# A cross network of six layers: bias load on GpSimd's queue with early bias products, and tail weights laid by copies

## The chip, the cores and the metric

The kernel runs on one core of a Trainium2 chip. The metric is the device time of one execution in microseconds, the median of several runs. A core has a matrix engine (TensorE, PE in the profile), a vector engine (VectorE, DVE), an activation engine (ScalarE, ACT), GpSimd (POOL) and SyncE (SP), which only issues transfers. DMA transfers can be issued from SP, ACT and GpSimd; each has a queue of its own.

## The reference

`x0` is 4096 x 416, `ws` is 6 x 416 x 416, `bs` is 6 x 416, all bf16. The output is the last `x`.

```python
def reference(x0, ws, bs):
    x = x0
    for l in range(ws.shape[0]):
        x = x0 * (x @ ws[l] + bs[l]) + x
    return x
```

## The kernel before, in words

**Layout.** Rows of the batch are worked in four passes `p` of 1024 rows, each as two blocks `blk` of 512. The features stand on partitions, so `x` is kept transposed. The 416 features are three chunks of 128 (index `k` as input, `m` as output) and a tail of 32. The tail of a pass's 1024 rows is packed on 128 partitions as four groups of 32, each group holding 256 rows (`x0t_sb`, `xt_sb`), so the 32 tail rows of a weight matrix must stand four times, once on each group's partitions: that is `w3_sb[:, l, :]`. The tail-to-tail part of the weights, 32x32, stands four times on the diagonal of a 128x128 matrix of zeros, `wc_sb[:, l, :]`.

**Biases.** PSUM keeps the sum of all layers' products, and `x` after layer l is x0 times (1 + all products so far + all biases so far). The sums of the biases come out of seven small products: `bsa_sb` (a row of ones and the six rows of `bs`) against the 7x6 triangle `u_sb`. They land in PSUM bank 7 and DVE copies them to `cb_sb` (L562); every later step on DVE and ACT reads it as its scalar, and `cl_sb` on GpSimd (L275) is made from it for the last layer.

**Steps of a layer.** `n = p*6 + l`. PE does `main(p, l, 0, n)` (chunk to chunk, block 0), `tail` (tail to chunks, L464; tail to tail, L398 with `wc_sb`; chunks to tail, L485) and `main(p, l, 1, n)`. DVE multiplies the results by `x0` (L579, L588), ACT and GpSimd share one chunk (L661, L285), and ACT copies the tail's other order (L627) and the next layer's `wc_sb` blocks (`corner`, L623). All order is written out by hand: each engine has its own list of instructions and waits on counting semaphores.

**The start**, around which the change lies. PE's list begins with `idle(28)`, matmuls on constants with no use for their result, then a wait for four set-up instructions of GpSimd (`s_setup`), and then `first()`:

- `turn(c)` for c = 0, 1, 2: twelve transposes (L316) of the first 512 rows, which wait for the two loads of `xin_sb`, the one on SP's queue, the other on ACT's.
- `biases()`: the seven products, which wait for `s_bs`, the load of `bs`.
- chunk k = 0 of layer 0 for block 0 (L388), which waits for the weights `s_w0[k]` and for DVE's copies of the turned rows into `x0T_sb` (L557, `s_ev`).
- two transposes of the tail (L359), which wait for GpSimd's packing `xtn_sb` (L262).
- `four_tails()`: one matmul of `rep_sb`, a 32x128 matrix of four identities side by side, with `w30_sb`, the 32 tail rows of layer 0's weights. It puts four copies of them in PSUM; ACT copies these to `w3_sb[:, 0, :]` (L630, `s_w30`), and then ACT and GpSimd copy two diagonal blocks of `wc_sb` each (L623 and L272, `s_wc` and `s_wc0`).
- chunks k = 1 and k = 2. Then `tail(0, 0, 0)` begins, with L464.

For layers 1 to 5 the four copies of the tail rows come from a DMA with a broadcast source (L174).

ACT's queue issues, in this order: second half of `xin_sb`, `xtb_sb` (tails of rows 512 to 1023), `bs`, `w30_sb`. GpSimd issues no DMA; its list begins with the memset of `ones_sb`, the row of ones, `ident`, `u_sb`, `rep_sb` and the zeros of `wc_sb`. SP's queue issues the first half of `xin_sb`, the three chunks of layer 0's weights, a transposing load of rows 512 to 1023, then the other weights and passes.

Of the kernel before, what the change touches and what calls it, by code (L numbers as in the profile page):

```python
# [7 lines left out]
ALU = mybir.AluOpType  # L8
ACTF = mybir.ActivationFunctionType


def bass_standalone__dcn_v2_cross__recsys_kernel(
# [13 lines left out]
    B, D = x0.shape  # L26
    L = ws.shape[0]
    DF = 384
    DR = D - DF
# [10 lines left out]
    with ExitStack() as es:  # L40
        block = es.enter_context(nc.Block())

        def sb(name, shape, dt=BF16):
            return es.enter_context(nc.sbuf_tensor(name, shape, dt))

        w_sb = sb("w_sb", [128, L, 3, D])
        w3_sb = sb("w3_sb", [128, L, D])
        w30_sb = sb("w30_sb", [DR, D])
        rep_sb = sb("rep_sb", [DR, 128])
        wc_sb = sb("wc_sb", [128, L, 128])  # L50
        x0T_sb = sb("x0T_sb", [128, 3, B])
        x0t_sb = sb("x0t_sb", [128, NP, 2, NT])
# [15 lines left out]
        ones_sb = sb("ones_sb", [128, 128])  # L68
        bsa_sb = sb("bsa_sb", [L + 1, D])
        u_sb = sb("u_sb", [L + 1, L])  # L70
        cb_sb = sb("cb_sb", [128, 4, L], FP32)
        ps = es.enter_context(nc.psum_tensor("ps", [128, 8, NB], FP32))
# [14 lines left out]
        def swapped(ap):  # L87
# [1 line left out]
            return [  # L89
                (ap[64 - 64 * h:128 - 64 * h, 1, :], ap[64 * h:64 * h + 64, 0, :]) for h in range(2)  # L90
            ]

        def blocks(l):

            gs = [slice(32 * g, 32 * g + 32) for g in range(4)]
            return [(wc_sb[g, l, g], w3_sb[g, l, DF:D]) for g in gs]

        def four(l):

# [8 lines left out]
        s_ones, s_setup, s_g = sem("s_ones"), sem("s_setup"), sem("s_g")  # L108
# [128 lines left out]

        @block.gpsimd
        def _(pool):
            pool.memset(ones_sb[:, :], 1.0).then_inc(s_ones, 1)  # L240
            pool.memset(bsa_sb[0:1, :], 1.0).then_inc(s_setup, 1)
            pool.wait_ge(s_ones, 1)
            pool.affine_select(
                out=ident[:, :], in_=ones_sb[:, :], pattern=[[-1, 128]],
                compare_op=ALU.is_equal, fill=0.0, base=0, channel_multiplier=1,
            ).then_inc(s_setup, 1)
            pool.affine_select(
                out=u_sb[:, :], in_=ones_sb[0:L + 1, 0:L], pattern=[[1, L]],
                compare_op=ALU.is_ge, fill=0.0, base=1, channel_multiplier=-1,
            ).then_inc(s_setup, 1)  # L250
            pool.affine_select(
                out=rep_sb[:, :].rearrange("f (g e) -> f g e", e=DR),
                in_=ones_sb[0:DR, :].rearrange("f (g e) -> f g e", e=DR),
                pattern=[[0, 4], [-1, DR]], compare_op=ALU.is_equal, fill=0.0, base=0,
                channel_multiplier=1,
            ).then_inc(s_setup, 1)
            pool.memset(wc_sb[:, :, :], 0.0).then_inc(s_g, 1)

            for h, src in enumerate((xin_sb[:, :, DF:D], xtb_sb[:, :, :])):
                for x in (s_xin, (s_xtb,))[h]:  # L260
                    pool.wait_ge(x, 16)
                pool.tensor_copy(  # L262
                    out=xtn_sb[:, 0, :, :].rearrange(
                        "b c (h k f) -> b c h k f", h=2, f=DR
                    )[:, :, :, h, :],
                    in_=src.rearrange("b (h c) f -> b c h f", c=2),
                ).then_inc(s_xtp, 1)
            pool.wait_ge(s_xtp, 2)
            pool.wait_ge(s_g, 1)
            pool.wait_ge(s_w30, 1)  # L270
            for o, i in blocks(0)[2:]:
                pool.tensor_copy(out=o, in_=i).then_inc(s_wc0, 1)  # L272
            pool.wait_ge(s_wc0, 2)
            pool.wait_ge(s_cb, 1)
            pool.tensor_scalar(  # L275
                out=cl_sb[:, :, :], in0=cb_sb[:, :, L - 1:L], scalar1=-1.0, scalar2=None,
                op0=ALU.add,
            ).then_inc(s_cl, 1)
            for p in range(NP):
                for l in range(L):  # L280
                    n = p * L + l
                    if n == N1:
                        continue
                    pool.wait_ge(s_act, n + 1)
                    pool.tensor_tensor(  # L285
                        out=xdst(p, l, 0, 2), in0=t_sb[:, n % 2, :], in1=x0c(p, 0, 2),
                        op=ALU.mult,
                    ).then_inc(s_pl, 1)

            pool.wait_ge(s_xr, 16)  # L290
            for i, j in enumerate((2, 3)):
                pool.wait_ge(s_tt, i + 1)
                pool.tensor_tensor(
                    out=o_sb[:, (NP - 1) * TT + j, :], in0=t_sb[:, i, 0:D], in1=xr_sb[:, j, :],
                    op=ALU.mult,
                ).then_inc(s_op, 1)

        @block.tensor
        def _(pe):

            def idle(n):
                ones = nc.const_aps.tensor(1.0, [128, 128], BF16)
                for _ in range(n):
                    pe.matmul(ps[:, 0, 0:128], lhsT=ones, rhs=ones, start=True, stop=True)  # L304

            idle(28)
            pe.wait_ge(s_setup, 4)
            def at(c, j):

                return 4 if (c, j // 2) == (0, 1) else (2, 3, 6)[c]  # L310
# [1 line left out]
            def turn(c):  # L312
# [7 lines left out]
                    if c == 0 and j == 1:  # L320
                        ins.then_inc(s_inT, 1)
                ins.then_inc(s_inT, 1)

            def four_tails():

                pe.wait_ge(s_wt[0], 16)
                whole(ps[:, 3, 0:D], rep_sb[:, :], w30_sb[:, :], True, True).then_inc(s_inT, 1)

            def biases():
                pe.wait_ge(s_bs, 16)  # L330
# [13 lines left out]

            def first():

                for c in range(3):
                    turn(c)
                biases()
                for k in range(3):  # L350
                    pe.wait_ge(s_w0[k], 16)
                    pe.wait_ge(s_ev, k + 2)
                    for m in range(3):
                        for o, x in pieces(0, m, xsrc(0, 0, 0, k)):
                            whole(o, w_sb[:, 0, k, m * 128:(m + 1) * 128], x, k == 0, False)
                    if k == 0:
                        pe.wait_ge(s_xtp, 2)
                        for c in range(2):
                            ins = pe.transpose(  # L359
                                out=psT[:, 2, c * 128:(c + 1) * 128],  # L360
                                in_=xtn_sb[:, 0, c, :], identity=ident[:, :],
                            )
                        ins.then_inc(s_inT, 1)
                        pe.wait_ge(s_ev, 3)
                        four_tails()

            def pieces(blk, m, x):

# [18 lines left out]
            def whole(out, lhsT, rhs, start, stop):  # L387
                return pe.matmul(  # L388
                    out, lhsT=lhsT, rhs=rhs, start=start, stop=stop, skip_group_check=True
                )  # L390
# [54 lines left out]
            def tail(p, l, n):  # L445
                if n == 0:
                    pe.wait_ge(s_ev, 5)
                    pe.wait_ge(s_cb, 1)
                    pe.wait_ge(s_w30, 1)
                elif l == 0:  # L450
                    pe.wait_ge(s_x0t[p], 16)
                elif n < L:
                    pe.wait_ge(s_wt[l], 16)
# [19 lines left out]
                ins.then_inc(s_pe, 1)  # L473

                if n == 0:
                    pe.wait_ge(s_wc0, 2)
                if n < L:
                    pe.wait_ge(s_wc, 4 * n + 2)
                columns(ps_tail, wc_sb[:, l, :], xt[:, 0, :], start=False, stop=False)

                if n == 0:
# [70 lines left out]

        @block.vector
        def _(dve):
            for i, (c, j0, j1) in enumerate(((0, 0, 2), (0, 2, 4), (1, 0, 4), (2, 0, 4))):
                dve.wait_ge(s_inT, i + 1)
                dve.tensor_copy(  # L557
                    out=x0T_sb[:, c, j0 * 128:j1 * 128],
                    in_=psT[:, (2, 4, 3, 6)[i], j0 * 128:j1 * 128],
                ).then_inc(s_ev, 1)  # L560
            dve.wait_ge(s_inT, 5)
            dve.tensor_copy(  # L562
                out=cb_sb[:, :, :],
                in_=ps[:, 7, D:D + 32].rearrange("p (c e) -> p c e", e=8)[:, :, 0:L],
            ).then_inc(s_cb, 1)
            dve.wait_ge(s_inT, 6)
            dve.tensor_copy(out=x0t_sb[:, 0, 0, :], in_=psT[:, 2, 0:NT]).then_inc(s_ev, 1)
            dve.wait_ge(s_ev, 5)
# [37 lines left out]
        def _(act):  # L606
# [3 lines left out]
            act.dma_start(  # L610
                xtb_sb[:, :, :], x0[NB:2 * NB, DF:D].rearrange("(j b) d -> b j d", b=128)
            ).then_inc(s_xtb, 16)
            act.dma_start(bsa_sb[1:L + 1, :], bs[:, :]).then_inc(s_bs, 16)
            act.dma_start(w30_sb[:, :], ws[0, DF:D, :]).then_inc(s_wt[0], 16)

            act.wait_ge(s_ones, 1)
            act.activation(out=act_sb[:, :], in_=ones_sb[:, 0:1], func=ACTF.Identity)

            def corner(l):
                if l > 0:  # L620
                    act.wait_ge(s_wt[l], 16)
                for o, i in blocks(l)[:2 if l == 0 else 4]:
                    act.activation(out=o, in_=i, func=ACTF.Copy).then_inc(s_wc, 1)  # L623

            def other(ap):
                for o, i in swapped(ap):
                    act.activation(out=o, in_=i, func=ACTF.Copy).then_inc(s_dup, 1)  # L627

            act.wait_ge(s_inT, 7)
            act.activation(  # L630
                out=w3_sb[:, 0, :], in_=ps[:, 3, 0:D], func=ACTF.Copy
            ).then_inc(s_w30, 1)
            act.wait_ge(s_g, 1)
            act.wait_ge(s_w30, 1)
            corner(0)

            def sums(n):

# [76 lines left out]
```

## Time and profile before

| what | value |
|---|---|
| median of 3 runs | 129.96 us (129.84 to 130.22) |
| profiled execution | 130.26 us |
| its span | 128.5 us |
| PE busy | 124.4 us (97% of the span) |
| DVE busy | 92.3 us (72%) |
| ACT busy | 45.9 us (36%) |
| POOL busy | 32.0 us (25%) |

The span is the stretch in which the profile shows work; the rest of the profiled execution's time, 1.76 us, lies around it. Engine names are those above; PEld is the loading of the matrix engine's weights, which overlaps its matmuls. `L398` is line 398 of the kernel. Matmuls are pipelined, so the duration of one is longer than the distance from its start to the start of the next. Durations come from one profiled execution, the median from unprofiled runs of the same kernel.

### The profile page before, as it was taken

To read this page: it belongs to the slowest core of one execution; us is meant where nothing else is said; L and a number is where in the kernel's file an instruction comes from. 1 tells how busy PE (TensorE), PEld (TensorE's weight loads), DVE (VectorE), ACT (ScalarE), POOL (GpSimd) and SP (SyncE) were. 2 spreads that over 40 slices of the span, in tenths; PEclk is the share of its full clock that TensorE was granted. 3 is DMA by queue.
4 is the path that set the end of the run, shared out by engine and by line. 5 is a ranking of instruction groups with operands and counts; after the bars stand their busy time and mean duration, and the time that the engine had idled before them with its cause. 6 is when DMAs were issued, how large, how long until landed. Compare 5 with 4: busy or idle time off the path is not lost.

```text
span 128.5 us, 5801 instructions
## 1 busy us (share of the span) xinstructions
PE 124.4 (97%) x2929; PEld 66.2 (52%) x2402; DVE 92.3 (72%) x152; ACT 45.9 (36%) x101; POOL 32.0 (25%) x40
## 2 busy tenths in 40 slices
PE   7999999999999999999999999999999999999990
PEld 7654554555445545545545545545545545546660
DVE  0439669669669669669679678688687697696482
ACT  1345446436404314314404224224214224225920
POOL 6123303303303203213113123123023033033050
PEclk9999999999999999999999999999999999999999
DMA  3979659665969940496300968000000857000026
GB/s 107 267 196 246 171 118 112 123 66 113 116 197 163 122 88 15 85 145 181 114 15 10 133 122 265 5 0 5 5 10 15 161 122 233 5 5 0 0 67 203
DMA packets 35463, 13.27 MB, mean 103 GB/s; under 512 B 26826, under 2 KB 35440, under 8 KB 35440
## 3 DMA queue, kind: packets, MB, share of 16 engines
q1 hardware_dynamic: 34436, 12.52, 48.7%
q10 hardware_dynamic: 1004, 0.38, 1.1%
q8 instruction: 21, 0.34, 1.1%
q14 instruction: 2, 0.02, 0.0%
HBM read 3.99 MB, written 3.41 MB: 58 GB/s over the span
## 4 chain that ended last, share of the span: by engine, by line
PE 97%; DVE 0%; issue 0%
PE ps L398 61%; PE ps L378 11%; PE ps L464 8%; PE ps L388 7%; PE ps L485 6%; PE ps L304 2%; PE ps L316 1%; DVE o_sb L600 0%; PE ps L528 0%; PE ps L332 0%; PE ps L338 0%; PE ps L359 0%
## 5 line engine op out<-in xcount | busy, mean ns | idle before, releaser
L579 DVE SCALAR_TENSOR_TENSOR xT_sb<-ps,cb_sb,x0T_sb 128x512 bf16<-128x512 f32 x100 | 69.3, 743 | 22.5 <-PE ps L464 22.5
L398 PE MATMUL ps<-xT_sb,w_sb 128*32 128x512 bf16 (+1 forms) x1380 | 75.7, 343 | 0.0
L398 PEld LDWEIGHTS ps<-xT_sb,w_sb 128*32 128x32 bf16 x1380 | 37.1, 97 | 35.0 <-issue 8.1
L285 POOL TENSOR_TENSOR xT_sb<-t_sb,x0T_sb 128x512 bf16<-128x512 f32 x20 | 23.3, 1163 | 72.0 <-ACT t_sb L661 72.0
L661 ACT ACTIVATE t_sb<-ps,cb_sb 128x512 f32<-128x512 f32 x23 | 15.8, 687 | 60.0 <-PE ps L464 60.0
L378 PE MATMUL ps<-xT_sb,w_sb 128*32 128x256 bf16 x444 | 26.6, 273 | 0.0
L627 ACT ACTIVATE xt_sb<-xt_sb 64x256 bf16<-64x256 bf16 x38 | 15.8, 415 | 9.8 <-DVE xt_sb L588 9.3
L398 PE MATMUL ps<-x0T_sb,w_sb 128*32 128x512 bf16 (+1 forms) x252 | 14.1, 344 | 0.0
L579 DVE SCALAR_TENSOR_TENSOR xo_sb<-ps,cb_sb,x0T_sb 128x512 bf16<-128x512 f32 x15 | 10.4, 743 | 3.3 <-PE ps L464 3.3
L398 PEld LDWEIGHTS ps<-x0T_sb,w_sb 128*32 128x32 bf16 x252 | 6.7, 97 | 6.5 <-issue 1.5
L464 PE MATMUL ps<-xt_sb,w_sb 32*128 32x256 bf16 x228 | 9.6, 271 | 0.0
L485 PE MATMUL ps<-xT_sb,w_sb 128*32 128x256 bf16 x228 | 9.5, 273 | 0.0
L588 DVE SCALAR_TENSOR_TENSOR xt_sb<-ps,cb_sb,x0t_sb 128x256 bf16<-128x256 f32 x20 | 9.5, 475 | 0.0
L464 PEld LDWEIGHTS ps<-xt_sb,w_sb 32*128 32x128 bf16 x228 | 4.2, 92 | 6.2 <-issue 6.1
L285 POOL TENSOR_TENSOR xo_sb<-t_sb,x0T_sb 128x512 bf16<-128x512 f32 x3 | 3.5, 1164 | 11.2 <-ACT t_sb L661 11.2
L485 PEld LDWEIGHTS ps<-xT_sb,w_sb 128*32 128x32 bf16 x228 | 6.1, 96 | 0.1
L398 PE MATMUL ps<-xt_sb,wc_sb 128*32 128x256 bf16 x76 | 5.6, 283 | 0.0
L623 ACT ACTIVATE wc_sb<-w_sb 32x32 bf16<-32x32 bf16 x22 | 5.0, 227 | 0.6
L388 PE MATMUL ps<-w_sb,xT_sb 128*128 128x416 bf16 x24 | 5.0, 339 | 0.0
L378 PE MATMUL ps<-x0T_sb,w_sb 128*32 128x256 bf16 x84 | 5.0, 273 | 0.0
L600 DVE SCALAR_TENSOR_TENSOR o_sb<-ps,xr_sb 128x416 bf16<-128x416 f32 x6 | 3.3, 585 | 2.4 <-PE ps L528 2.3
L557 DVE COPY x0T_sb<-ps 128x256 bf16<-128x256 bf16 (+1 forms) x4 | 1.4, 358 | 4.5 <-PE ps L316 4.3
(54 smaller groups left out, 48.3 us busy)
## 6 DMA issues: line engine op xcount, KB each, us to landing
out_dram<-o_sb SPq DMA_DIRECT2D x3, 832.0 KB, 4.9
w_sb<-in_ws_dram SPq DMA_DIRECT2D x5, 312.0 KB, 5.5
w_sb<-in_ws_dram SPq DMA_DIRECT2D x8, 104.0 KB, 3.4
xr_sb<-in_x_dram SPq DMA_DIRECT2D x1, 832.0 KB, 6.4
out_dram<-o_sb SPq DMA_DIRECT2D x3, 208.0 KB, 2.1
xin_sb<-in_x_dram SPq DMA_DIRECT2D x1, 208.0 KB, 3.0
xin_sb<-in_x_dram ACTq DMA_DIRECT2D x1, 208.0 KB, 3.3
x0T_sb<-in_x_dram SPq DMA_TRANSPOSE x13, 4.2
```

What stands on the lines that cost most here:

```text
L285: pool.tensor_tensor(out=xdst(p, l, 0, 2), in0=t_sb[:, n % 2, :], in1=x0c(p, 0, 2), op=ALU.mult,).then_inc(s_pl, 1)
L378: return pe.add_instruction(mybir.InstMatmult(name="I-%d" % (1000000 + count[0]), engine=mybir.EngineType.PE, start_tensor_calc=start, sto ...
L388: return pe.matmul(out, lhsT=lhsT, rhs=rhs, start=start, stop=stop, skip_group_check=True)
L398: ins = pe.matmul(out[c:c + 32, :], lhsT=lhsT[:, c:c + 32], rhs=rhs, start=start, stop=stop, skip_group_check=True, tile_position=(0, c),)
L464: ins = pe.matmul(part(blk, m, h ^ other), lhsT=w3_sb[32 * g:32 * g + 32, l, m * 128:(m + 1) * 128], rhs=xt[32 * g:32 * g + 32, other, :], ...
L485: ins = pe.matmul(ps_tail[32 * g:32 * g + 32, :], lhsT=w_sb[:, l, k, DF:D], rhs=xsrc(p, l, g % 2, k)[:, (g // 2) * NT:(g // 2 + 1) * NT], ...
L579: dve.scalar_tensor_tensor(out=halves(xdst(p, l, blk, c)), in0=chunk2(blk, c), scalar=cb_sb[:, c, l:l + 1], in1=halves(x0c(p, blk, c)), op ...
L588: dve.scalar_tensor_tensor(out=tdst(p, l), in0=ps_tail, scalar=cb_sb[:, 3, l:l + 1], in1=x0t_sb[:, p, 0, :], op0=ALU.add, op1=ALU.mult,).t ...
L600: dve.scalar_tensor_tensor(out=o_sb[:, (NP - 1) * TT + j, :], in0=ps[:, BANK[j], 0:D], scalar=1.0, in1=xr_sb[:, j, :], op0=ALU.add, op1=AL ...
L623: act.activation(out=o, in_=i, func=ACTF.Copy).then_inc(s_wc, 1)
L627: act.activation(out=o, in_=i, func=ACTF.Copy).then_inc(s_dup, 1)
L661: act.activation(out=halves(t_sb[:, n % 2, :]), in_=chunk2(0, 2), func=ACTF.Identity, bias=cb_sb[:, 2, l:l + 1],).then_inc(s_act, 1)
```

## The change

The load of `bs` is issued first on GpSimd's queue, no longer third on ACT's, so `w30_sb` becomes ACT's third transfer. The seven bias products stand ahead of the turns, the copy of `cb_sb` is the first in DVE's list, and there are 24 idle products instead of 28. `rep_sb`, `four_tails` and ACT's copy out of PSUM are gone: as soon as `w30_sb` is there, ACT copies it to the first three groups of `w3_sb` and DVE to the fourth, and GpSimd copies all four blocks of `wc_sb` for layer 0 straight from `w30_sb`, each behind the one before. ACT's `corner` is used for layers 1 to 5 only.

```diff
@@ gpsimd
+            pool.dma_start(bsa_sb[1:L + 1, :], bs[:, :]).then_inc(s_bs, 16)
             pool.memset(ones_sb[:, :], 1.0).then_inc(s_ones, 1)
...
-            pool.affine_select(
-                out=rep_sb[:, :].rearrange("f (g e) -> f g e", e=DR),
...
-            pool.wait_ge(s_w30, 1)
-            for o, i in blocks(0)[2:]:
-                pool.tensor_copy(out=o, in_=i).then_inc(s_wc0, 1)
-            pool.wait_ge(s_wc0, 2)
+            pool.wait_ge(s_wt[0], 16)
+            for g in range(4):
+                gs = slice(32 * g, 32 * g + 32)
+                pool.tensor_copy(out=wc_sb[gs, 0, gs], in_=w30_sb[:, DF:D]).then_inc(s_wc0, 1)
+                pool.wait_ge(s_wc0, g + 1)
@@ tensor
-            idle(28)
-            pe.wait_ge(s_setup, 4)
+            idle(24)
+            pe.wait_ge(s_setup, 3)
...
-            def four_tails():
-
-                pe.wait_ge(s_wt[0], 16)
-                whole(ps[:, 3, 0:D], rep_sb[:, :], w30_sb[:, :], True, True).then_inc(s_inT, 1)
...
             def first():
 
+                biases()
                 for c in range(3):
                     turn(c)
-                biases()
...
-                        pe.wait_ge(s_ev, 3)
-                        four_tails()
@@ tail
-                    pe.wait_ge(s_w30, 1)
+                    pe.wait_ge(s_w30, 4)
...
-                    pe.wait_ge(s_wc0, 2)
-                if n < L:
-                    pe.wait_ge(s_wc, 4 * n + 2)
+                    pe.wait_ge(s_wc0, 4)
+                elif n < L:
+                    pe.wait_ge(s_wc, 4 * n)
@@ vector
+            dve.wait_ge(s_inT, 1)
+            dve.tensor_copy(
+                out=cb_sb[:, :, :],
+                in_=ps[:, 7, D:D + 32].rearrange("p (c e) -> p c e", e=8)[:, :, 0:L],
+            ).then_inc(s_cb, 1)
             for i, (c, j0, j1) in enumerate(((0, 0, 2), (0, 2, 4), (1, 0, 4), (2, 0, 4))):
-                dve.wait_ge(s_inT, i + 1)
+                dve.wait_ge(s_inT, i + 2)
...
-            dve.wait_ge(s_inT, 5)
-            dve.tensor_copy(
-                out=cb_sb[:, :, :],
...
+            dve.wait_ge(s_wt[0], 16)
+            dve.tensor_copy(out=w3_sb[96:128, 0, :], in_=w30_sb[:, :]).then_inc(s_w30, 1)
@@ scalar
-            act.dma_start(bsa_sb[1:L + 1, :], bs[:, :]).then_inc(s_bs, 16)
             act.dma_start(w30_sb[:, :], ws[0, DF:D, :]).then_inc(s_wt[0], 16)
...
-            act.wait_ge(s_inT, 7)
-            act.activation(
-                out=w3_sb[:, 0, :], in_=ps[:, 3, 0:D], func=ACTF.Copy
-            ).then_inc(s_w30, 1)
-            act.wait_ge(s_g, 1)
-            act.wait_ge(s_w30, 1)
-            corner(0)
+            act.wait_ge(s_wt[0], 16)
+            for g in range(3):
+                act.activation(
+                    out=w3_sb[32 * g:32 * g + 32, 0, :], in_=w30_sb[:, :], func=ACTF.Copy
+                ).then_inc(s_w30, 1)
```

More of the change, by code (lines that the diff above doesn't have):

```diff
@@ L48, in bass_standalone__dcn_v2_cross__recsys_kernel @@
         w30_sb = sb("w30_sb", [DR, D])
-        rep_sb = sb("rep_sb", [DR, 128])
         wc_sb = sb("wc_sb", [128, L, 128])
@@ L91, in swapped @@
             ]
-        def blocks(l):
-            gs = [slice(32 * g, 32 * g + 32) for g in range(4)]
-            return [(wc_sb[g, l, g], w3_sb[g, l, DF:D]) for g in gs]
         def four(l):
@@ L249, in _ @@
                 compare_op=ALU.is_ge, fill=0.0, base=1, channel_multiplier=-1,
-            ).then_inc(s_setup, 1)
-            pool.affine_select(
-                out=rep_sb[:, :].rearrange("f (g e) -> f g e", e=DR),
-                in_=ones_sb[0:DR, :].rearrange("f (g e) -> f g e", e=DR),
-                pattern=[[0, 4], [-1, DR]], compare_op=ALU.is_equal, fill=0.0, base=0,
-                channel_multiplier=1,
             ).then_inc(s_setup, 1)
@@ L560, in _ @@
                 ).then_inc(s_ev, 1)
-            dve.wait_ge(s_inT, 5)
-            dve.tensor_copy(
-                out=cb_sb[:, :, :],
-                in_=ps[:, 7, D:D + 32].rearrange("p (c e) -> p c e", e=8)[:, :, 0:L],
-            ).then_inc(s_cb, 1)
+            dve.wait_ge(s_wt[0], 16)
+            dve.tensor_copy(out=w3_sb[96:128, 0, :], in_=w30_sb[:, :]).then_inc(s_w30, 1)
             dve.wait_ge(s_inT, 6)
@@ L619, in corner @@
             def corner(l):
[L620 to L623, printed above, removed]
+                act.wait_ge(s_wt[l], 16)
+                for g in range(4):
+                    gs = slice(32 * g, 32 * g + 32)
+                    act.activation(
+                        out=wc_sb[gs, l, gs], in_=w3_sb[gs, l, DF:D], func=ACTF.Copy
+                    ).then_inc(s_wc, 1)
             def other(ap):
@@ L627, in other @@
                     act.activation(out=o, in_=i, func=ACTF.Copy).then_inc(s_dup, 1)
-            act.wait_ge(s_inT, 7)
-            act.activation(
-                out=w3_sb[:, 0, :], in_=ps[:, 3, 0:D], func=ACTF.Copy
-            ).then_inc(s_w30, 1)
-            act.wait_ge(s_g, 1)
-            act.wait_ge(s_w30, 1)
-            corner(0)
+            act.wait_ge(s_wt[0], 16)
+            for g in range(3):
+                act.activation(
+                    out=w3_sb[32 * g:32 * g + 32, 0, :], in_=w30_sb[:, :], func=ACTF.Copy
+                ).then_inc(s_w30, 1)
             def sums(n):
```

## The prediction

> **What bounds the kernel now.** I read part 1 of the page first (PE busy 97% of the span), then the list of waits. In that list PE waits for no other engine after 0.8 us; its only other idle time is 0.2 us "issue". So the end is set by how much work stands in PE's queue, and by when PE reaches the first layer's tail products. The change touches nothing after those products except two thresholds, so I followed the chain of waits over the first 14 us. Columns: start us, duration us, what.
>
> ```profile
> 0.83 3.15 PE ps L304 x28
> 3.97 1.40 PE ps L316 x12
> 5.37 0.17 PE ps L332 x3
> 5.54 0.12 PE ps L338 x2
> 5.66 1.13 PE ps L388 x4
> 6.79 0.11 PE ps L359 x2
> 6.90 0.28 PE ps L388
> 7.18 0.16 issue
> 7.34 1.25 PE ps L388 x7
> 8.59 0.44 PE ps L464 x12
> ```
>
> These are, in order: idle products, turns of the first 512 rows, biases (L332, L338), chunk k=0 of layer 0, turns of the tail, the matmul that lays the tail weights (the lone L388 at 6.90) with 0.16 us behind it, chunks k=1 and 2, and the tail products. Everything on this list is PE's own work, so what leaves it shortens the span.
>
> Next I read the DMA issues, for the landing times (last column, us from issue).
>
> ```profile
> xin_sb<-in_x_dram SPq DMA_DIRECT2D x1, 208.0 KB, 3.0
> xin_sb<-in_x_dram ACTq DMA_DIRECT2D x1, 208.0 KB, 3.3
> ...
> out_dram<-o_sb SPq DMA_DIRECT2D x1, 104.0 KB, 2.0
> ...
> xtb_sb<-in_x_dram ACTq DMA_DIRECT2D x1, 32.0 KB, 3.4
> w_sb<-in_ws_dram ACTq DMA_DIRECT2D x1, 26.0 KB, 3.2
> ```
>
> In the timeline the two xin loads are issued at 0.79 and 0.80, so they land at 3.79 and 4.10: the turns cannot start before about 3.9, nor reach their third matmul before 4.2. Size hardly shows (26 KB takes as long as 104 KB), load does: the 2.0 is for a transfer at the very end.
>
> Last I read PE's timeline for matmul durations, since the sum depends on PE's pace.
>
> ```profile
> 5.59 0.61 PE L388 MATMUL ps<-x0T_sb,w_sb 128*128 128x512 bf16 x1
> ```
>
> ```profile
> 7.34 0.38 PE L388 MATMUL ps<-x0T_sb,w_sb 128*128 128x512 bf16 x1 [0.16 <-issue]
> ```
>
> The same matmul takes 0.61 us at 5.6 and 0.38 us at 7.3. The second one of k=0 (start 5.99) takes 581 ns and the ones from 6.41 on are short. Start to start it is 0.42 us per 512 columns early and 0.21 late. So PE doubles its pace at about 6.5 us, although the granted clock on the page is 9 in every slice. Time saved before 6.5 us is worth half, because the work that moves into it runs at half pace.
>
> **The change, part by part.**
>
> *Tail weights.* The lone L388 at 6.90 and the 0.16 us behind it go: 7.34 - 6.90 = 0.44 us off PE's queue, at full pace. Chunk k=1 then follows the tail's turns directly; its needs are long met (the w0 loads land at 4.5, 5.2 and 5.8; the last x0T copy on DVE ended at 5.83). Removed as well: ACT's copy of 517 ns (L630), GpSimd's affine_select of 299 ns and ACT's two corner copies of 228 ns; all were beside PE's work.
>
> Added are three ACT copies 32x416, one DVE copy, and two more 32x32 copies on GpSimd. None has a row. For ACT, 64x256 takes 415 ns (L627) and 128x416 out of PSUM 517, so three take 1.2 to 1.6 us; I take 1.6, by the equal length. For DVE 222 ns (L570) to 424 ns (L557); I take 0.4. GpSimd's 32x32 takes 206 ns; four of them with a wait between each, 0.8 to 1.4 us; I take 1.4. They start when w30 has landed. Its issue moves up one place in ACT's queue, from 2.53 to 1.85, so it lands at 1.85 + 3.2 = 5.05 (5.73 if the earlier issue gains nothing). ACT ends at 6.7 to 7.4, GpSimd at 6.5 to 7.2, DVE by 6.3. PE needs them at L464, about 8.1 in the new kernel, and at the wc product 0.44 later: cover 0.6 us or more, so I cost them at nothing. If the cover is gone, each us late is a us of span. Behind DVE's new wait for w30 stand the copies of x0t: these wait for the tail's turns (6.94 before) anyway. Behind GpSimd's stand cl (used at the end) and the product of 9.91. Behind ACT's stands t_sb of 9.14. What is next late is x0t: from the end of the tail's turns to the end of its two copies 6.90 to 7.73 = 0.83 us, while PE now reaches L464 1.25 us after the turns. That is 0.4 us of cover left.
>
> *Biases.* L332 and L338, 0.17 + 0.12 = 0.29 us, move from behind the turns to ahead of them. There PE only waited: 24 idle products end at 0.83 + 24 x 0.1125 = 3.53, xin lets the turns start at 3.9. So 0.29 us leave the stretch 5.37 to 5.66, at half pace: 0.145 us. The copy of cb on DVE (170 ns) comes earlier, beside the turns.
>
> The price is that all turns now stand behind the wait for the bias transfer. It is issued on GpSimd at 0.79 instead of on ACT at 1.85. Call T its landing; turns start at the later of 3.97 and T + 0.1 + 0.29. The two agree at T = 3.58; beyond that each us costs half a us, so the gain is 0.44 + 0.5 x (3.87 - T): 0.59 up to 3.58, 0.39 at 3.97, 0.28 at 4.19, nothing at 4.75.
>
> No row shows a transfer issued by GpSimd. Bounds: 0.79 + 2.0 = 2.8 from the lightest row, 0.79 + 3.4 = 4.2 from xtb; whatever GpSimd adds of its own comes on top and belongs to the first rival. The rows of 3.2 to 3.4 stood second to fourth in their queues behind 208 KB; this transfer is 4.9 KB and first in its own, so I go to the middle, T = 3.5, leaning to 3.8 for a slower start. That is a gain of 0.48 to 0.59; I take 0.5.
>
> The Trainium skill (DMA: Bandwidth & Descriptors, Anatomy of one DMA) gives a GpSimd transfer about 2.0 us fixed plus bytes over 436 GB/s, which would be T = 2.8 and the whole 0.59 us; the same page (Latency and other measured facts) gives its first byte 1 us against 0.6 us for SP and ACT, which speaks against this move by 0.4 us. No run here shows either yet.
>
> *GpSimd's queue.* The issue stands ahead of ones, the memset of bsa, ident, u_sb, the memset of wc and the two xtn copies. u_sb ended at 1.67 + 0.18 = 1.85 before; biases need it at 3.53. That covers 1.7 us of issue time. ACT's issues take 0.32 to 0.66 us, so I cost it at nothing. The xtn copies (4.20) have 1.7 us: wc's memset ended at 2.79, less 0.30 for the select that goes.
>
> *The rest.* SP's order is as before. Four idle products fewer cost nothing by themselves. w1 landed at 5.76 + 2.8 = 8.6 and is needed at 11; the load of layer 2 lands at 11.3 and is needed at 15. So nothing is waiting to take the gain back.
>
> *Sum.* Profiled execution: 130.26 us, span 128.5 and 1.76 around it. Less 0.5: 129.76. It stands 0.30 above the median of the runs, 129.96, so the forecast for the median is 129.45.
>
> **The rivals.**
>
> *Late biases.* GpSimd's transfer lands after 3.97, and the turns wait. For it: no row for such a transfer, and DMA share over 0.9 from 2 us on. Against: size and place. Between 3.97 and 5.55 the result lies within 0.3% (at 4.5: 0.13 gained, 129.8). Past 5.55 it is slower by more: at T = 6.0 the turns start at 6.39, run at full pace (two tail turns take 0.11 us, so twelve 0.66), k=0 ends 0.64 later at 7.7 against 6.79, and 0.9 - 0.44 is about half a us lost, 130.5.
>
> *The pace comes later: slower.* PE had worked without a hole from 0.83 to 6.54 when it sped up, 5.7 us. Now between 3.53 and 3.97 there are only seven 6-column products and a pause. If that hole starts the count anew, the pace doubles at 3.97 + 5.7 = 9.7. Then k=0 takes 1.28 from 5.37, the tail's turns 0.23, k=1 and 2 take 1.28 each, L464 starts at 9.44 and ends at 10.0 against 9.03: one us slower, 130.95. It decides from the point at which the hole is counted as idle, and a later T widens the hole. For it: the duration rows above. Against: seven products fill part of the hole, and 12 turns of 128 columns follow.
>
> The Trainium skill (TensorE: Matmul & The Clock Gate, The HAM clock gate) says that the array starts at half clock and is let go after a busy window of about 3.4 us that runs freely. By it a missed window would move 6.54 to 9.95 and the time to about 131.1; one busy window fits the trace, in which 3.1 to 6.5 was filled and the stretch before only from 0.83.
>
> *The cover is thinner than worked out.* Three cross-partition ACT copies, GpSimd's four or the x0t chain end after PE is there. For it: no rows for these forms. Against: 0.4 to 1 us of cover. Half a us late cancels the gain, 129.95; beyond 0.9 us it is slower.
>
> *It doesn't do what it says.* The 0.16 us could belong to the change from turns to chunks rather than to the matmul removed. Then 0.28 + 0.145 remains, 129.55: still faster.
>
> **How the numbers follow.** What a measurement can tell here is about 0.3%, 0.39 us. Forecast, 129.2 to 129.57 (the low end for a pace that doubles before 5.4, when the biases' whole 0.29 counts, 0.73 in all): 0.50. Late biases 0.23: within 0.3% 0.16, slower 0.07. Later pace 0.15. Thin cover 0.12: same 0.07, slower 0.05. So faster 0.50, same 0.23, slower 0.27. Leaving out the later pace together with the worst late cases would leave out more than 2 in 10, so the range reaches to it: 129.2 to 131.1.
>
> **What would show it** (lines as numbered before). Right: the chain begins with 24 of L304, biases at about 3.5, turns at 3.9 to 4.0, k=0 at about 5.4, no lone L388, L464 at about 8.1 instead of 8.59, and no wait of PE for ACT there. Wrong: a gap of PE before the biases (T), matmuls 128x512 of 0.6 us after 6.6 us (pace), or L464 and the wc product starting on an ACT, GpSimd or DVE release (cover).

## The result, and the profile after

The changed kernel is slower: 131.75 us median (131.30 to 132.18) against 130.01 before (four runs; 129.96 was the median of the first three), ratio 1.0139 with a 95% interval of 1.0115 to 1.0163. Its profiled execution took 131.86 us with a span of 130.1 us. The forecast was 129.45 us with a range of 129.2 to 131.1; a loss of 1.7 us lies outside it. Here and below a ratio leaves out every run more than 1.5% above the fastest of its kernel (among them one of 254.76 us with the hole alone and one of 147.57 us with two and two copies), while medians and ranges are of all runs.

First the chain of waits of the changed kernel (start us, duration us, what), the counterpart of the one shown before. The line numbers have moved: L306 are the turns, L317 and L323 the biases, L371 the chunks, L344 the tail's turns, L447 the tail products.

```profile
1.30 3.69 DMA bsa_sb<-in_bs_dram
4.99 0.14 issue
5.13 0.21 PE ps L317 x3
5.34 0.11 PE ps L323 x4
5.45 0.78 PE ps L306 x12
6.23 0.11 issue
6.34 0.84 PE ps L371 x4
7.18 0.21 PE ps L344 x2
7.39 2.56 PE ps L371 x8
9.95 0.67 PE ps L447 x10
```

The chain now begins with a transfer: the biases land at 4.99 and everything on PE stands behind them. Then two things are to be seen. The twelve turns take 0.78 us where they took 1.40, so PE is at its full pace by 5.4, earlier than before. But chunks k=1 and 2 take 2.56 us where they took 1.25, so PE is back at half pace. The table by stretches shows the same; its columns are the stretch and its length, then the busy time and count of PE, PEld, DVE, ACT and POOL, then the granted TensorE clock (1.00 is full), the DMA share and GB/s.

```profile
5.00:7.00 2.00, 1.76 (x24) 1.34 (x25) 1.45 (x6) 0.88 (x2) 0.70 (x4) 1.00 1.04 184
7.00:10.00 3.00, 3.00 (x16) 1.37 (x17) 0.89 (x4) 0.76 (x2) 0.44 (x2) 0.50 0.69 179
10.00:12.00 2.00, 2.00 (x48) 1.14 (x48) 1.23 (x3) 0.74 (x2) 0.48 (x1) 0.90 0.95 269
```

The granted clock is 0.50 from 7.0 to 10.0, and 0.90 as a mean of the next 2 us: 0.4 us more at half. So the half clock lasts from 7.0 to 10.4, 3.4 us. PE is busy all through it: the busy column does not tell.

This fall belongs to the profiled execution. Half a clock for 3.4 us of 130.1 gives a mean granted clock of 0.987, and 0.986 is on record for it; the other three executions have 1.00, 1.00 and 0.997 and took 131.30, 131.64 and 132.18 us. They lost as much without a fall of that length. The experiments show another way to lose it, one that the clock column does not show; whether these three lost it so is not on record.

PE's own list of waits names what came before that:

```profile
PE ps L317 <- DMA bsa_sb<-in_bs_dram: 1.6, 1, 1.6
```

That hole, from 3.55 to 5.13, is the only wait of PE for another engine or a transfer in the whole span. The landings (last column, us from issue):

```profile
w_sb<-in_ws_dram ACTq DMA_DIRECT2D x1, 26.0 KB, 4.2
bsa_sb<-in_bs_dram POOLq DMA_DIRECT2D x1, 4.9 KB, 3.7
```

Piece by piece, before against after, from the start of the turns to the end of the tail products (L464, now L447):

| piece | before | after | difference |
|---|---|---|---|
| turns start | 3.97 | 5.45 | +1.48 |
| turns, with the issue gap behind | 1.40 | 0.89 | -0.51 |
| biases behind the turns | 0.29 | none | -0.29 |
| chunk k=0 | 1.13 | 0.84 | -0.29 |
| tail's turns | 0.11 | 0.21 | +0.10 |
| four_tails and the gap behind | 0.44 | none | -0.44 |
| chunks k=1 and 2 | 1.25 | 2.56 | +1.31 |
| tail products | 0.44 | 0.67 | +0.23 |
| end of the tail products | 9.03 | 10.62 | +1.59 |

From there to the end of the span it is 128.5 - 9.03 = 119.47 us before and 130.1 - 10.62 = 119.48 after. Between these two executions all of the loss arises in the first 11 us and nothing is given back later.

### The profile page after: what moved, and what is told of

Its sections match the earlier page's. It is cut to its first block, busy times and chain, and to the rows that moved or that the text cites. A ratio compares the mean times of both kernels' runs of the same rounds, so it can differ in the third digit from the quotient of the medians.

```text
span 130.1 us, 5791 instructions
## 1 busy us (share of the span) xinstructions
PE 124.5 (96%) x2925; PEld 65.7 (50%) x2397; DVE 92.5 (71%) x153; ACT 46.6 (36%) x101; POOL 32.9 (25%) x42
## 4 chain that ended last, share of the span: by engine, by line
PE 94%; DMA 3%; issue 1%; DVE 0%; POOLq 0%
PE ps L381 60%; PE ps L361 11%; PE ps L447 8%; PE ps L371 7%; PE ps L468 6%; DMA bsa_sb<-in_bs_dram 3%; PE ps L306 1%; DVE o_sb L585 0%; PE ps L511 0%; PE ps L344 0%; PE ps L317 0%; PE ps L323 0%; POOLq L686 0%
## 5 line engine op out<-in xcount | busy, mean ns | idle before, releaser
L564 DVE SCALAR_TENSOR_TENSOR xo_sb<-ps,cb_sb,x0T_sb 128x512 bf16<-128x512 f32 x15 | 10.4, 744 | 3.3 <-PE ps L447 3.3
L447 PE MATMUL ps<-xt_sb,w_sb 32*128 32x256 bf16 x228 | 9.6, 271 | 0.0
L447 PEld LDWEIGHTS ps<-xt_sb,w_sb 32*128 32x128 bf16 x228 | 4.2, 92 | 6.2 <-issue 6.1
L371 PE MATMUL ps<-w_sb,xT_sb 128*128 128x416 bf16 x24 | 5.0, 339 | 0.0
L608 ACT ACTIVATE wc_sb<-w_sb 32x32 bf16<-32x32 bf16 x20 | 4.5, 226 | 0.5
```

Source lines behind the costliest of these rows:

```text
L371: return pe.matmul(out, lhsT=lhsT, rhs=rhs, start=start, stop=stop, skip_group_check=True)
L447: ins = pe.matmul(part(blk, m, h ^ other), lhsT=w3_sb[32 * g:32 * g + 32, l, m * 128:(m + 1) * 128], rhs=xt[32 * g:32 * g + 32, other, :], ...
L564: dve.scalar_tensor_tensor(out=halves(xdst(p, l, blk, c)), in0=chunk2(blk, c), scalar=cb_sb[:, c, l:l + 1], in1=halves(x0c(p, blk, c)), op ...
L608: act.activation(out=wc_sb[gs, l, gs], in_=w3_sb[gs, l, DF:D], func=ACTF.Copy).then_inc(s_wc, 1)
```

## The experiments

Two theories: the loss is the *wait* for the late biases, or it is the *pace* that PE loses by standing still. A third question is whether the tail half brought its 0.44 us. Each time is a median; each ratio is to the kernel before on the same chip. A hole is a stretch in which PE does nothing.

**The tail half alone.** From the changed kernel: load of `bs` back on ACT ahead of `w30`, products behind the turns, 28 idle products.

> Only the tail-weight half of the change (three copies on ACT, one on DVE, four on GpSimd, no four_tails matmul); the biases stay as before: loaded on ACT third, products behind the turns, 28 idle products. If the tail half is worth the 0.44 us that the prediction gave it, 129.55 us, and L464's place in the chain comes at 8.15 instead of 8.59. If the copies end too late (the thin-cover rival), 130.0 or more, with the tail products released by ACT, DVE or GpSimd. If the loss of the change sits in this half, about 131.

Measured 129.87 against 129.87, ratio 0.9998 (0.9982 to 1.0013): no gain that can be told. Its list of waits between 7 and 9 us shows a wait that was not there before (L446 are the tail products, L619 the copies of w30):

```profile
PE ps L446 <- ACT w_sb L619: 0.2, 1, 0.2
```

ACT's three copies ran from 6.02 to 7.72, because w30 landed near 6.0. The copies are now what PE waits for: the thin-cover rival, in its mild form. The wait is 0.2 us, half of the 0.44 us.

**The bias half alone.** From the kernel before: load on GpSimd, `biases()` ahead of the turns, 24 idle products.

> Only the bias half: load on GpSimd first, seven products ahead of the turns, 24 idle products; four_tails and its matmul stay. If the whole loss is in this half and the tails gain 0.44, this is 131.75 + 0.44 = 132.2 us, with a hole of PE of 1.5 us before the products and a stretch of 3.4 us at half pace after it. If the loss is shared with the tail half, 131.3 or less.

Measured 132.0, ratio 1.0131 (1.0092 to 1.0170). As far as these intervals tell, the whole loss is in this half. In its profile (131.47 us) the biases land at 4.81, the turns run from 5.28 at half pace (1.39 us), and chunk k=0 too (1.28); chunks k=1 and 2 are at full pace (1.25). So the pace doubles late here and does not fall again.

**Products behind the turns, load still on GpSimd.**

```diff
 (changed kernel)
-                biases()
                 for c in range(3):
                     turn(c)
+                biases()
```

> The changed kernel with the bias products put back behind the turns and 28 idle products; the load stays on GpSimd and the tails are laid by copies. If the loss comes from the turns standing behind the late load, 129.5 us, although the load still lands near 5.0. If the transfer on GpSimd harms by itself (the weight loads landed 0.6 to 0.8 us later beside it), 130.0 or more, with PE waiting for w0 or ACT for w30.

Measured 129.62, ratio 0.9978 (0.9964 to 0.9992): slightly faster than before. The same late transfer on the same queue does no harm when nothing stands behind it.

**The hole filled.** `idle(24)` becomes `idle(42)` in the changed kernel.

> The changed kernel with 42 idle products instead of 24, so that PE has no hole while it waits for the biases (42 end at 4.6 us or later, by the pace). The load still lands near 5.0 and the turns still start at 5.4 or later. If the loss is the pace that the hole costs, most of it goes: about 130.0 us and no half-pace stretch after 7 us. If the loss is the wait itself, the time stays at 131.3 to 131.8.

Measured 130.31, ratio 1.0039 (1.0021 to 1.0057). The chain of waits (L294 the idle products; the other lines as in the changed kernel):

```profile
0.83 4.43 PE ps L294 x42
5.26 0.16 PE ps L317 x3
5.42 0.14 PE ps L323 x4
...
7.35 1.30 PE ps L371 x8
8.65 0.44 PE ps L447 x12
```

The biases start at 5.26, even later than in the changed kernel, and chunks k=1 and 2 take 1.30 us instead of 2.56. Eighteen matmuls of no use take the ratio from 1.0139 to 1.0039: 1.0% of 130, 1.3 us, was the pace. What remains, 130.31 against 129.62 with the products behind, is 0.7 us. It is not the wait for the load alone. Here the load landed at 4.8 (issued at 1.30, 3.5 us to landing), and the biases stood behind the last idle product; then PE waited 0.3 us for DVE's copies of the turned rows, which the quick turns had outrun.

**The hole alone.** The kernel before with `idle(14)`; no transfer is moved.

> The kernel before with 14 idle products instead of 28 and nothing else: PE stops at 2.4 us and starts the turns at 3.97 as ever, a hole of 1.5 us like that of the changed kernel, but without a later transfer. If the hole costs by the pace that comes later, 130.6 to 131.4 us, with matmuls 128x512 of 0.6 us after 6.6. If only the wait for the biases costs, 129.9.

Measured 131.72, ratio 1.0139 (1.0117 to 1.0160): as much as the whole change cost. Its chain:

```profile
0.79 2.93 DMA xin_sb<-in_x_dram
3.71 0.14 issue
3.85 1.44 PE ps L316 x12
...
7.18 3.04 PE ps L388 x9
10.22 0.44 PE ps L464 x12
```

PE stops at 2.48, so the hole is 1.4 us. The turns start no later than before (3.85), and the nine matmuls from the tail-weight one on take 3.04 us instead of 0.28 + 0.16 + 1.25. One of the forms shown before, now at 7.56:

```profile
7.56 0.61 PE L388 MATMUL ps<-x0T_sb,w_sb 128*128 128x512 bf16 x1
```

0.61 us, where it was 0.38 at 7.34. Nothing but idle matmuls was taken away, so the pace depends on them. The clock column does not show it. The stretch from 7 to 10 us reads 1.00 here, where the changed kernel's reads 0.50, at the same pace of PE:

```profile
7.00:10.00 3.00, 3.00 (x11) 1.13 (x9) 0.74 (x3) 0.97 (x3) 0.64 (x3) 1.00 0.83 214
```

In these traces the column shows a fall from full pace, not a pace that has yet to double; that one is read from the durations of matmuls.

**Half that hole.** The kernel before with `idle(21)`.

> The kernel before with 21 idle products instead of 28: PE stops at 3.2 and the turns start at 3.97, a hole of 0.7 us, half of that with 14, which cost 1.8 us. If the pace is lost in proportion to the hole, 130.8. If a short hole is tolerated, 129.9 to 130.2. If any hole starts the count anew, 131.5 or more.

Measured 131.83, ratio 1.0180 (1.0139 to 1.0221), runs from 130.87 to 133.16; the medians alone, 131.83 and 129.77, give 1.016. A hole of 0.8 us cost no less than one of 1.4. The loss is not in proportion to the hole. The profiled execution, 130.87, is the fastest of the six: its turns and chunk k=0 are at half pace (1.47 and 1.39 us), and the pace doubles within the nine matmuls behind, which take 1.78 us.

**The load on ACT, products still ahead.** From the changed kernel:

```diff
-            pool.dma_start(bsa_sb[1:L + 1, :], bs[:, :]).then_inc(s_bs, 16)
...
+            act.dma_start(bsa_sb[1:L + 1, :], bs[:, :]).then_inc(s_bs, 16)
             act.dma_start(w30_sb[:, :], ws[0, DF:D, :]).then_inc(s_wt[0], 16)
```

> The changed kernel with the load of the biases back on ACT's queue, third, issued at 1.85; the products stay ahead of the turns, 24 idle products. If GpSimd's queue is what makes the load late, it lands at 4.4 or before, and the time is about 130.3. If any small transfer lands late at this point, because of the others under way, it lands at 1.85 + 3.2 to 3.5, that is 5.05 to 5.35, and the time is 131.7 to 132.

The chain answers on the landing:

```profile
1.85 3.40 DMA bsa_sb<-in_bs_dram
5.25 0.14 issue
```

5.25, inside what the second theory gave. This is the slowest of its twelve executions, 133.16. The median is 131.54, a little under the 131.7 expected, with runs from 129.99 to 133.16; the medians alone, against 129.92, give 1.012, and the ratio, by the rule given with the result, is 1.0071 (1.0036 to 1.0105). GpSimd's queue is not the only way to be late: third on ACT the load is later still. That does not clear GpSimd, where the load stood first and still took 3.69 us from its issue, against 3.40 here.

**The load first on SP.** The changed kernel with the load ahead of the first half of xin on SP's queue.

> The changed kernel with the load of the biases first on SP's queue, ahead of the first half of xin; products ahead of the turns, 24 idle products. If such a load lands 3 us or more after its issue on any queue, it is there at 3.8 to 4.2, the hole of PE is 0.3 to 0.7 us, xin lands near 4.3, and the time is 130 to 131, most of it by the pace. If it lands about 2 us after its issue, as the lightest rows of the trace, there is no hole and the time is about 129.6.

In its timeline PE goes on from the idle products to the biases with no wait, and waits 0.38 us for xin instead:

```profile
3.48 0.23 PE L317 MATMUL ps<-u_sb,bsa_sb 7*128 7x6 bf16 x3
...
4.21 0.84 PE L306 MATMUL ps<-ident,xin_sb 128*128 128x128 bf16 x12 [0.38 <-DMA xin_sb<-in_x_dram]
```

So the load, issued at 0.78, was there by 3.5: at most 2.7 us, against 3.4 behind two others on ACT and 3.7 first on GpSimd, where it was issued at 1.30. Queue and moment of issue change together, so which of the two makes the difference stays open. The median is 129.66, ratio 0.9996 (0.9965 to 1.0028), with runs from 129.08 to 131.73.

**Who limits the tail half.** The tail half alone, with two copies on ACT and two on DVE:

```diff
-            dve.tensor_copy(out=w3_sb[96:128, 0, :], in_=w30_sb[:, :]).then_inc(s_w30, 1)
+            for g in (2, 3):
+                dve.tensor_copy(
+                    out=w3_sb[32 * g:32 * g + 32, 0, :], in_=w30_sb[:, :]
+                ).then_inc(s_w30, 1)
...
-            for g in range(3):
+            for g in range(2):
```

> The tail half alone (as in the first experiment: biases as before) with two copies of w30 on ACT and two on DVE instead of three and one. In the first experiment ACT's third copy ended at 7.72 and the tail products waited 0.19 us for it. If that chain takes the gain of the tail half, ACT now ends at 7.2, nothing waits, and the time is 129.5 to 129.65 against 129.87. If the tail half has no gain for another reason, 129.87 again.

Measured 129.80 against 129.92, ratio 0.9974 (0.9955 to 0.9992), runs from 129.16. ACT ended at 7.0 and PE did not wait for it. This fits the copies as the floor (the lowest run of the tail half alone was 129.69), and a tail half worth about 0.3 us without it, though the intervals of the two experiments overlap.

**w30 second on ACT's queue**, with two and two copies, products behind the turns, load on GpSimd.

> The version that the runs point to: biases loaded on GpSimd but their products behind the turns, 28 idle products, tails by two copies on ACT and two on DVE, and w30 second on ACT's queue, ahead of xtb. If the chain from w30's landing to ACT's last copy is what limits the tail half, it now ends by 6.7 and the time is about 129.45. If xtb, now third, comes late for GpSimd's packing and the tail's turns, 129.7 or more.

Measured 129.82, ratio 0.9997 (0.9981 to 1.0013): no gain, for the second of the reasons named. Waits between 5 and 8 us:

```profile
POOL xtn_sb L251 <- DMA xtb_sb<-in_x_dram: 1.8, 1, 1.8
...
PE ps L344 <- POOL xtn_sb L251: 0.6, 1, 0.6
```

xtb, third, landed 4.2 us after its issue instead of 3.4, and the tail's turns waited for GpSimd's packing. The place in the queue was handed on, not won.

**Both small gains together**: products behind the turns, load on GpSimd, w30 third, two and two copies.

> Biases loaded on GpSimd with their products behind the turns (as in the run that gave 129.62), and tails by two copies on ACT and two on DVE (as in the run that gave 129.80); w30 third on ACT, xtb second. ACT should end by 7.1 instead of 7.6. If that floor is what the two runs have in common, 129.45 to 129.6. If both gains are one and the same, or lie elsewhere, 129.6 to 129.8.

Measured 129.67, ratio 0.9987 (0.9969 to 1.0006): inconclusive; the two gains did not show as a sum.

**The version the runs point to**: load first on SP, products ahead, 28 idle products, two and two copies.

> The version that the runs point to: the load of the biases first on SP's queue, products ahead of the turns, 28 idle products instead of 24 (they end at 3.98, the products at 4.3, and xin lands at 4.1, so PE has no hole), tails by two copies on ACT and two on DVE. If the slow runs of the version with 24 idle products (131.0 to 131.7 beside 129.1 to 130.0) are the hole's, they are gone and the time is 129.2 to 129.5. If they come from the transfers, the spread stays and the median is 129.6 or more.

Measured 129.47 against 130.06, ratio 0.9962 (0.9940 to 0.9984), runs from 129.09 to 130.14. It beats the kernel before, and with it the changed one; the runs above 131 are gone. About half of the gain is not in the span, though. With the load first on SP, the time of an execution exceeds its span by 1.41 to 1.59 us in all 24 executions of the two versions; in every other kernel here it does by 1.68 to 1.90. The median span is 128.0 us here against 128.3 of the kernel before beside it, and with the load first on SP and 24 idle products 128.25 against 128.0. What shortens the part outside the span is open. Its profiled execution (129.94) shows what is next: between 6 and 20 us

```profile
ACT wc_sb L611 <- DMA w_sb<-in_ws_dram: 2.4, 1, 2.4
...
PE ps L381 <- ACT wc_sb L611: 0.5, 1, 0.5
```

ACT waits for the tail weights of layer 1, which landed at 12.4, and PE for ACT's blocks of them. The tail products start at 7.37, where they start at 8.04 with two and two copies and the biases behind; most of that lead, 0.5 us, goes into this wait.

## Why the prediction was wrong, point by point

The step that failed is the price of a late bias load. The sum took T = 3.5 and let each us beyond 3.58 cost half a us, with the doubling of the pace held at 6.5 us. The load landed at 4.99, and the hole that it left took the pace as well: in the profiled execution chunks k=1 and 2 took 2.56 us instead of 1.25.

**Tail weights: right that four_tails and its gap go, wrong on the cover.** The 0.44 us left PE's chain, as the table shows, gap included. But cover of "0.6 us or more" rested on w30 landing at 5.05, or 5.73 at the latest. It was issued at 1.85 as foreseen and landed at 6.05: 4.2 us, not 3.2. The earlier issue gained nothing: fourth on the queue, in the tail half alone, it landed near 6.0 too. The ACT copies were sized well (1.69 against 1.6), so they ended at 7.8. In the changed kernel PE did not wait for them, because it came so late; in the tail half alone it did, for 0.2 us.

**T, the term that failed first.** The sum had T = 3.5, with an upper bound of 4.2 and GpSimd's own share on top. Measured: 4.99. Two parts: the issue began at 1.30, not 0.79, and lasted 0.75; and from its start to landing it took 3.69, not 2.7. The bet that a 4.9 KB transfer, first in its own queue, is quicker than its neighbours under load failed on GpSimd, where the row of xtb (3.4) was the better guide; first on SP it held (at most 2.7). On top of the upper bound of 4.2 came 0.5 us in the issue and 0.3 us from issue to landing; what comes on top had been left to the first rival. The first rival was there, at 0.23.

**The pace, which made the loss.** By the sum's own formula T = 4.99 costs little: 0.44 + 0.5 x (3.87 - 4.99) is a loss of 0.12 us. That formula held the doubling fixed at 6.5 us. The hole alone, in the kernel before, costs 1.8 us; filling it gives back 1.3 us of the change's loss. This was the second rival, with the right sign, at 0.15; its size, one us for a hole of 0.44, is about half of the 1.8 and 2.1 us that holes of 1.4 and 0.8 us cost. The error was to price the two rivals as separate: a late T is what makes the hole, so the first brought the second with it. "Four idle products fewer cost nothing by themselves" belongs to the same error: with the load first on SP and 24 of them three of twelve runs took 131.0 to 131.7, with 28 (and other copies) none did.

What the hole does is not quite the "count anew" of the prediction. In the changed kernel's profiled execution the pace had doubled by 5.4 and halved again from 7.0 to 10.4; in the bias half alone and in the kernel before with 14 idle products it simply doubled later. Common to all is that a stretch with a hole was followed by half pace. Why it takes the one form or the other is not shown. The Trainium skill (TensorE: Matmul & The Clock Gate, The HAM clock gate) has a window of about 3.4 us that runs freely against the kernel. The stretch at half clock here lasted 3.4 us, and the spread of single runs (129.99 to 133.16 with the load on ACT) fits a window whose phase differs from run to run, though no run set that phase on purpose. The same page of the Trainium skill wants about a window of idle before the clock falls; here a hole of 1.6 us was enough to halve it.

**What held.** The load moved GpSimd's chain by 1.3 us, within its cover: `u_sb` ended at 3.12 instead of 1.85, before 3.53. x0t and `wc_sb` were never late, and w1 and the later weights did not hold PE in the changed kernel. Whether moving the biases ahead pays when they are there in time is not settled: the median span of the last version, 128.0 us, is 0.3 below that of the kernel before beside it, and with two and two copies and the biases behind it is 0.2 below (128.0 against 128.2).

## What to carry to other kernels

Ahead of the first real work PE should not stand still: a wait put in front of the queue costs by the delay and, here, about 1.3 us more in pace; a few idle matmuls that cover the wait buy the pace back. When a step is moved ahead of everything else, its transfer must go ahead as well, and a landing time is to be taken from the rows of the same moment, however small the transfer. Two rivals that share a cause are not to be priced apart: if the first comes, the second comes with it.

## What the runs showed of the hardware that was not expected

- A pause of PE of 0.8 us at about 3.5 us costs as much (ratio 1.018) as one of 1.4 us (1.014).
- GpSimd's first transfer was issued half a us later than the first ones of SP and ACT (1.30 against 0.79 and 0.81) and kept GpSimd for 0.75 us; it then landed as late as a third transfer on ACT (4.99 against 5.25).
- The third transfer on ACT's queue landed at 5.0 to 6.05 us whatever it was (4.9 to 32 KB): 3.4 us after issue for the biases, 3.2 to 4.2 for w30, 4.2 for xtb.
- The granted clock of a stretch can read 1.00 at half pace: 0.61 us for a 128x512 matmul at 7.56 us in the kernel before with 14 idle products, against 0.38 at full pace.
- With the load of `bs` first on SP, the time exceeds the span by about 1.5 us instead of about 1.75, in 24 of 24 executions; the cause is open.
- A copy of 32x416 takes 0.26 to 0.29 us on DVE and 0.56 us on ACT.
